# Regrouping the TensorE work of an attention round: both value products together, then every plain float32 matmul, then both fill steps

## Chip, cores and metric

One core of one Trainium2 chip. The metric is the device time of one execution in microseconds (us); of several runs the median is given. A difference is called faster or slower when it is over 0.2% (4.3 us), and no change inside that.

## What is computed

Sink-and-window attention over 4 batches, 8 heads, 768 positions of width 64, then a dense mixture of 8 experts whose gate is normalised over tokens and experts in turn:

```
scores = scale * q @ k.T                      # kept: the first 4 positions, and the last 128
a = softmax(where(keep, scores, -1e9))
x = (a @ v) laid out as 3072 tokens x 512
P = exp(x @ w_gate - max); 8 times: normalise P over experts, then over tokens
out = sum over e of P[:, e] * (relu(x @ w1[e]) @ w2[e])      # F = 1024
```

Everything is float32. Most large products are made as three matmuls in the faster float32r type, from a high part and a low part of each operand; transposes and the gate's products use plain float32.

## The kernel before

The attention is cut into 48 units: 4 batches, 6 blocks of 128 queries, 2 halves of 4 heads. A loop over `n` (L719 on) works on five units at once, each in another state. One turn of that loop is called a round here. TensorE's order in it is the order of the code (`tc.manual_schedule(engines={PE})`); the other engines' orders come from a scheduler, which places their instructions by what TensorE's order makes ready. In a round TensorE does, by line:

- L468, `scores(n + 1)`: 12 float32r matmuls into the PSUM banks `st0` to `st3`, one bank for each head. VectorE adds the mask and takes the maximum (L471), ScalarE takes the exponential (L474), VectorE inverts the sums (L475, L476), GpSimd scales the rows (L478).
- L527, `values(n - 1, 0)` and `values(n - 1, 1)`: 7 float32r matmuls each, into one tile `O` (two PSUM buffers, shared with the gate). `store_x` copies `O` out in two halves, L539, one on ScalarE and one on VectorE, and every second unit stores a block of `x`.
- L433, `transpose_qk(n + 2)`: 4 plain float32 transposes into `st0`. ScalarE copies the high part (L437) and VectorE the low part (L438) into `KQ`, which the next round's scores read.
- L489, `transpose_p(n, 0)` and `(n, 1)`: 8 transposes of the scaled scores into `st1` and `st2`; `split` (L350) copies them out as a high part on ScalarE and a low part on VectorE into `PT`.
- L506, `transpose_sinks(n)`: one transpose into `st3`, copied out by ScalarE (L508).
- `gate_step()`: a quarter of a token tile's gate product, two TensorE passes of 8 columns (L557), with a copy by VectorE (L560) behind the fourth; or, for the first 1024 tokens, a third of a group's product (L568; then a copy `ls`, L573, and eight small passes that read it, L577, and L578).
- `run_fill(1)`: a piece of the mixture's first expert, to fill TensorE's time: either six matmuls of 256 columns (L606), after each second one of which the hidden part is taken by ScalarE (L611) and VectorE (L612), or three of 512 columns (L622). The two kinds take turns.

In a round where the first block of a batch is worked on, there are fewer of L527 and L489, since there is no previous block and no sinks. The fill's weights come by DMA and are split into high and low parts by L350 too (tiles `W1`, `W2f`, `W1f`), in a few rounds. After the attention come the rest of the fill and seven eighths of the mixture, L791, L1035 and L1350, which the change doesn't touch.

The next round's scores need four things: `st0` and `KQ` (L437, L438), `st1` and `st2` (both L350 of each) and `st3` (L508).

Of the kernel before, what the change touches and what calls it, by code (L numbers as in the profile page):

```python
# [229 lines left out]
def tile_sink_attention_moe(ctx: ExitStack, tc: tile.TileContext, q, k, v, wg, w1, w2, out):  # L230
# [4 lines left out]
    E, _, FF = w1.shape  # L235
# [18 lines left out]
    def f32(ap):  # L254
        return ap.bitcast(F32)
# [146 lines left out]
    def load_sinks(b):  # L402
        vs = seq[b] = att.tile([SK, D], F32, name="vs")
        for r0 in range(0, SK, NK):
            (nc.sync if b else nc.scalar).dma_start(vs[r0:r0 + NK, :], v[b, :, 0:SINK, :])

    def split_sinks(b):

        vm = att1.tile([SK, H, D], F32, name="vm")
        nc.gpsimd.tensor_tensor(vm, seq[b].unsqueeze(1).broadcast_to([SK, H, D]), bd.unsqueeze(2).broadcast_to([SK, H, D]), op=ALU.mult)  # L410
        VS = seq[b] = att.tile([SK, H * D], F32R, name="VS")
        vmf = vm.rearrange("p h d -> p (h d)")
        nc.gpsimd.tensor_scalar(VS, vmf, 1.0, 1.0, op0=ALU.mult, op1=ALU.mult)
        nc.gpsimd.tensor_sub(VS[2 * NK:], vmf[2 * NK:], f32(VS[2 * NK:]))

    def load_block(b, i):
        raws[b, i] = r = [att.tile([P, H, D], F32, name=nm) for nm in ("kr", "qr", "vr")]
        cuts = (0, HH, H) if (b, i) == (0, 0) else (0, H)
        for ts in (((r[0], k), (r[1], q)), ((r[2], v),)):
            for h0, h1 in zip(cuts, cuts[1:]):  # L420
                for t, src in ts:
                    nc.sync.dma_start(t[:, h0:h1, :], src[b, h0:h1, i * P:(i + 1) * P, :].rearrange("h p d -> p h d"))
# [88 lines left out]
    def values(n, pr):  # L511

        b, i, hh = units[n]
        u = us[n]
        if pr == 0:
            u["O"] = ps_o.tile([P, NP, 2, P], F32, name="O")
        cs = slice(pr * P, (pr + 1) * P)
        ops = []
        ws = (1,) if i == 0 else (0, 1)
        for j, w in enumerate(ws):  # L520
            V = us[n - 2 + 2 * w]["V"]
            for x_, y_ in ((0, 0), (0, 1), (1, 0)):
                ops.append((V[:, x_, cs], u["PT", pr][:, y_, j]))
        if i:
            ops.append((seq[b][:, hh * HH * D:][:, cs], u["PS"].unsqueeze(1).broadcast_to([SK, 2, P])))
        for j, (x_, y_) in enumerate(ops):
            nc.tensor.matmul(u["O"][:, pr], lhsT=x_, rhs=y_, start=(j == 0), stop=(j == len(ops) - 1))  # L527
        if pr == NP - 1:
            store_x(n)
# [51 lines left out]
    def gate_step():  # L581
        if gates and next(gates[0], 0) == 0:
            gates.pop(0)
            gate_step()
# [76 lines left out]
    def run_fill(k_):  # L661
        for _ in range(k_):
            next(fill, None)
# [53 lines left out]
    START = 5  # L717
    with tc.manual_schedule(engines={PE}):
        for n in range(-2, L + 3):  # L719
            on = lambda j: 0 <= j < L  # L720
            if on(n + 2):
                b, i, hh = units[n + 2]
                if hh == 0:
                    with (tc.high_priority() if n == -2 else nullcontext()):
                        load_block(b, i)
                    if i == 0:
                        load_sinks(b)
            if n == -2:
                nc.sync.dma_start(wg_raw, wg.rearrange("(k p) e -> p k e", p=P))
            if n == 2:  # L730
                with tc.issue_after(us[1]["split"][1]):
                    split_gate()
            gates += later
            later.clear()
            if on(n + 1):
                scores(n + 1, 0)
                scores(n + 1, 1)
            if on(n - 1):
                values(n - 1, 0)
            if n >= START:  # L740
                run_fill(1)
            gate_step()
            for j in (0, 1) if n == -2 else (n + 2,) if n >= 0 else ():
                if on(j):
                    transpose_qk(j)
            if on(n):
                transpose_p(n, 0)
                with (tc.issue_after(us[n - 1]["scaled"]) if n > 1 else nullcontext()):
                    split_v(n)
            gate_step()  # L750
            if on(n):
                transpose_p(n, 1)
            if on(n - 1):
                values(n - 1, 1)
            gate_step()
            if on(n) and units[n][1]:
                transpose_sinks(n)
            if on(n) and units[n][1:] == (0, 1):
                with tc.issue_after(us[n]["scaled"]):
                    split_sinks(units[n][0])  # L760
            if n >= START:
                run_fill(1)
            first_w1(n)
        while gates:
            gate_step()
# [760 lines left out]
```

## Time and profile before

| what | value |
|---|---|
| median of 3 runs | 2140.49 us (2140.0 to 2141.41) |
| profiled execution, its own time | 2140.46 us |
| its span on the core | 2138.7 us |
| TensorE busy, share of the span | 99% |
| VectorE, ScalarE, GpSimd busy | 72%, 41%, 35% |
| mean granted TensorE clock | 0.997 |

Between the span and the execution's own time lie 1.8 us, which no change inside the kernel moves. The rounds of attention fill the stretch from 6.5 to about 298 us. Matmuls are pipelined and their ends are modelled in the profile, so a row's duration holds its neighbour's too: how long something takes on TensorE is read from one start to the next. A wait is listed only where the gap is over 0.15 us.

### The profile page before, as it was taken

To read this page: it belongs to the slowest core of one execution; us is meant where nothing else is said; L and a number is where in the kernel's file an instruction comes from. 1 tells how busy PE (TensorE), PEld (TensorE's weight loads), DVE (VectorE), ACT (ScalarE), POOL (GpSimd) and SP (SyncE) were. 2 spreads that over 40 slices of the span, in tenths; PEclk is the share of its full clock that TensorE was granted. 3 is DMA by queue.
4 is the path that set the end of the run, shared out by engine and by line. 5 is a ranking of instruction groups with operands and counts; after the bars stand their busy time and mean duration, and the time that the engine had idled before them with its cause. 6 is when DMAs were issued, how large, how long until landed. Compare 5 with 4: busy or idle time off the path is not lost.

```text
span 2138.7 us, 31819 instructions
## 1 busy us (share of the span) xinstructions
PE 2120.3 (99%) x10501; PEld 1769.8 (83%) x10501; DVE 1538.8 (72%) x2821; ACT 881.9 (41%) x1867; POOL 750.4 (35%) x950
## 2 busy tenths in 40 slices
PE   8999999999999999999999999999999999999998
PEld 7898897888888888888888888888888888888887
DVE  8878868877777776766666666666657666666666
ACT  7777745444444444442333223332333223332322
POOL 7766643233232331232223222233323232233223
PEclk9999999999999999999999999999999999999999
DMA  7434326999999987686666666667866666666662
GB/s 184 95 84 101 86 80 230 314 307 312 294 309 293 310 290 251 216 282 205 204 192 201 208 192 205 203 200 262 297 204 196 199 207 194 200 207 189 205 197 85
DMA packets 397643, 453.83 MB, mean 212 GB/s; under 512 B 99680, under 2 KB 265760, under 8 KB 396576
## 3 DMA queue, kind: packets, MB, share of 16 engines
q1 hardware_dynamic: 397080, 451.57, 68.0%
q8 instruction: 86, 1.41, 0.3%
q14 instruction: 85, 0.70, 0.1%
q10 hardware_dynamic: 392, 0.16, 0.0%
HBM read 314.17 MB, written 137.46 MB: 211 GB/s over the span
## 4 chain that ended last, share of the span: by engine, by line
PE 94%; DVE 3%; ACT 1%; DMA 1%; issue 0%; POOL 0%; SPq 0%; ACTq 0%; DVEq 0%
PE c L791 40%; PE o L1350 20%; PE held L1350 8%; PE held L1035 7%; PE o L1035 7%; PE O L527 3%; PE st L468 2%; PE st L489 1%; PE o L622 1%; PE g L606 1%; ACT sc L474 1%; PE st L433 1%; DVE sc L471 0%; PE O L557 0%; PE st L606 0%
## 5 line engine op out<-in xcount | busy, mean ns | idle before, releaser
L817 ACT CAST hf<-w 128x512 fp32r<-128x512 f32 x448 | 265.0, 620 | 561.5 <-POOL w L1317 299.2
L1350 PE MATMUL o<-hf,W2q 128*128 128x512 f32 x1920 | 472.0, 389 | 0.0
L1350 PEld LDWEIGHTS o<-hf,W2q 128*128 128x128 f32 x1920 | 360.0, 188 | 75.5 <-DVE acc L1364 0.8
L791 PE MATMUL c<-T,W1q 128*128 128x512 f32 x1530 | 389.0, 389 | 0.2 <-DVE w L1298 0.2
L818 DVE TENSOR_TENSOR hf<-w,hf 128x512 fp32r<-128x512 f32 x448 | 330.4, 766 | 74.3 <-ACT hf L817 66.8
L791 PEld LDWEIGHTS c<-T,W1q 128*128 128x128 f32 x1530 | 286.7, 188 | 60.9 <-DVE w L1298 1.2
L1364 DVE TENSOR_TENSOR acc<-o,acc 128x512 f32<-128x512 f32 x298 | 204.6, 687 | 171.5 <-PE o L1350 171.5
L791 PE MATMUL c<-B,W1q 128*128 128x512 f32 x1134 | 278.3, 389 | 0.0
L1317 POOL TENSOR_TENSOR w<-w 128x512 f32<-128x512 f32 x64 | 82.7, 1292 | 493.2 <-DVE w L1299 486.6
L791 PEld LDWEIGHTS c<-B,W1q 128*128 128x128 f32 x1134 | 212.5, 188 | 44.0
L1298 DVE TENSOR_TENSOR w<-c,M 128x512 f32<-128x512 f32 x192 | 132.3, 689 | 138.8 <-PE c L791 133.1
L1294 ACT COPY M<-c 128x512 f32<-128x512 f32 x192 | 112.7, 587 | 250.4 <-PE c L791 250.3
L1350 PE MATMUL held<-hf,W2q 128*128 128x512 f32 x768 | 194.8, 389 | 0.0
L791 PE MATMUL c<-T,W1f 128*128 128x512 f32 x672 | 171.2, 390 | 0.2
L1035 PE MATMUL held<-W2f,h 128*128 128x512 f32 x672 | 171.1, 390 | 0.0
L1035 PE MATMUL o<-W2f,h 128*128 128x512 f32 x672 | 170.6, 389 | 0.1
L1350 PEld LDWEIGHTS held<-hf,W2q 128*128 128x128 f32 x768 | 144.0, 188 | 29.9
L1332 POOL TENSOR_TENSOR w<-w 128x512 f32<-128x512 f32 x64 | 105.7, 1651 | 176.2 <-DVE hf L818 176.2
L1035 PEld LDWEIGHTS o<-W2f,h 128*128 128x128 f32 x672 | 126.0, 188 | 27.0 <-DVE acc L1042 0.9
L791 PEld LDWEIGHTS c<-T,W1f 128*128 128x128 f32 x672 | 125.7, 188 | 27.1 <-ACT M L998 0.5
L1035 PEld LDWEIGHTS held<-W2f,h 128*128 128x128 f32 x672 | 125.8, 188 | 26.4 <-DVE W2f L818 0.5
L844 POOL TENSOR_TENSOR r<-r 128x256 f32<-128x256 f32 x27 | 20.1, 744 | 359.6 <-ACT M L998 210.0
(216 smaller groups left out, 3100.3 us busy)
## 6 DMA issues: line engine op xcount, KB each, us to landing
W2q<-w2s SPq DMA_DIRECT2D x448, 256.0 KB, 3.2
W1q<-w1s SPq DMA_DIRECT2D x444, 256.0 KB, 2.8
w1s<-W1f SPq DMA_DIRECT2D x56, 896.0 KB, 7.6
w2s<-WT SPq DMA_DIRECT2D x136, 256.0 KB, 3.4
r<-in_moe_w_dram SPq DMA_DIRECT2D x64, 512.0 KB, 4.0
w2s<-W2f SPq DMA_DIRECT2D x56, 256.0 KB, 4.8
PB<-psd SPq DMA_DIRECT2D x16, 512.0 KB, 4.2
w2s<-W2f SPq DMA_DIRECT2D x56, 128.0 KB, 6.5
```

The costliest lines, as they stand in the source:

```text
L468: nc.tensor.matmul(ps[h], lhsT=Q[r0:r0 + D, a, pr, :], rhs=K[r0:r0 + D, c, pr, :], start=(j == 0), stop=(j == 2))
L527: nc.tensor.matmul(u["O"][:, pr], lhsT=x_, rhs=y_, start=(j == 0), stop=(j == len(ops) - 1))
L791: nc.tensor.matmul(ps, lhsT=w1(a, k), rhs=x[:, b, k, :], start=(start and j == 0), stop=(stop and j == len(TERMS) - 1), skip_group_check=n ...
L817: nc.scalar.copy(dst[:, 0], src)
L818: at(1, lambda: nc.vector.tensor_sub(dst[:, 1], src, f32(dst[:, 0])))
L1035: nc.tensor.matmul(o, lhsT=h[c, th][:, a, off:off + P], rhs=W2F[n][:, w, c, :], start=(begin and c == 0 and j == 0), stop=(end and c == 1 ...
L1294: nc.scalar.copy(t, T["c2"])
L1298: nc.vector.tensor_add(w, T["c1"], T[m])
L1317: nc.gpsimd.tensor_sub(S3, T["A11"], T["A21"])
L1332: at(k, lambda: nc.gpsimd.tensor_sub(T["A11"], w, T["A11"]))
L1350: nc.tensor.matmul(o, lhsT=W2Q[part, n, m][:, a, k * P:(k + 1) * P], rhs=F[part, n, H_OF[m]][:, w, :], start=(j == 0 and (begin or not hol ...
L1364: nc.vector.tensor_add(sums[m, k], o, sums[m, k])
```

## The change

In each round `values(n - 1, 1)` moves up behind `values(n - 1, 0)`; the two `transpose_p` follow each other; the three gate steps, which stood at three places of the round, stand in a row behind the transposes; and the two fill steps, of which one stood behind the first values and one at the round's end, both stand at its end. No instruction is added or taken away. The PSUM banks that each use takes are the same.

```diff
             if on(n - 1):
                 values(n - 1, 0)
-            if n >= START:
-                run_fill(1)
-            gate_step()
+                values(n - 1, 1)
             for j in (0, 1) if n == -2 else (n + 2,) if n >= 0 else ():
                 if on(j):
                     transpose_qk(j)
@@
                 transpose_p(n, 0)
                 with (tc.issue_after(us[n - 1]["scaled"]) if n > 1 else nullcontext()):
                     split_v(n)
-            gate_step()
-            if on(n):
                 transpose_p(n, 1)
-            if on(n - 1):
-                values(n - 1, 1)
-            gate_step()
             if on(n) and units[n][1]:
                 transpose_sinks(n)
             if on(n) and units[n][1:] == (0, 1):
                 with tc.issue_after(us[n]["scaled"]):
                     split_sinks(units[n][0])
+            for _ in range(3):
+                gate_step()
             if n >= START:
-                run_fill(1)
+                run_fill(2)
             first_w1(n)
```

TensorE in a round with three gate steps, behind its scores. Before (`st_3397` is the bank for the new K and Q, `st_3404`, `st_3416` and `st_3438` those for the transposed scores and sinks; `g` and `o` are the fill's):

```order
L527 MATMUL O<-PT,V 128x256 x6
L527 MATMUL O<-PS,VS 128x256
L606 MATMUL g_3388<-B_163,W_719 128x256 x2
...
L557 MATMUL O<-wg_raw,xr 128x8
L433 MATMUL st_3397<-ident,kr 128x128
...
L489 MATMUL st_3404<-ident,sc 128x128 x4
L557 MATMUL O<-wg_raw,xr 128x8
L489 MATMUL st_3416<-ident,sc 128x128 x4
L527 MATMUL O<-PT,V 128x256 x6
L557 MATMUL O<-wg_raw,xr 128x8
L506 MATMUL st_3438<-ident,SS_172 96x128
L622 MATMUL o<-W2f,h_2390 128x512 x3
```

And now:

```order
L527 MATMUL O<-PT,V 128x256 x6
L527 MATMUL O<-PS,VS 128x256
L527 MATMUL O<-PT,V 128x256 x6
L527 MATMUL O<-PS,VS 128x256
L433 MATMUL st_3398<-ident,kr 128x128
...
L489 MATMUL st_3405<-ident,sc 128x128 x4
L489 MATMUL st_3416<-ident,sc 128x128 x4
L506 MATMUL st_3427<-ident,SS_172 96x128
L557 MATMUL O<-wg_raw,xr 128x8 x3
L606 MATMUL g_3435<-B_163,W_762 128x256 x2
...
L622 MATMUL o<-W2f,h_2437 128x512 x3
```

The second values moved ahead of all transposes, and the three gate steps (each row of L557 is two passes) became one run between the last transpose and the fill.

VectorE in a round in which a tile's fourth gate step and a split of the fill's weights (`W`) fall, behind the scores' maxima (`st` are the sums of the rows, `h` and `g` the fill's, `KQ`, `PT` and `xr` as above). Before:

```order
L475 TENSOR_SCALAR st<-st 128x2
L476 RECIPROCAL st<-st 128x2
L560 COPY Xt<-O 128x8
L475 TENSOR_SCALAR st<-st 128x2
L476 RECIPROCAL st<-st 128x2
L612 SCALAR_TENSOR_TENSOR h_3183<-g_3388,h_3183 128x256
L350 TENSOR_TENSOR W_3611<-r_3607,W_3611 128x512
L438 TENSOR_TENSOR KQ_174<-st_3503,KQ_174 128x2x2x128
L350 TENSOR_TENSOR PT<-st_3510,PT 128x512
L350 TENSOR_TENSOR PT<-st_3521,PT 128x512
L539 COPY xr<-O 64x256
```

And now:

```order
L475 TENSOR_SCALAR st<-st 128x2
L476 RECIPROCAL st<-st 128x2
L475 TENSOR_SCALAR st<-st 128x2
L476 RECIPROCAL st<-st 128x2
L539 COPY xr<-O 64x256
L438 TENSOR_TENSOR KQ_174<-st_3503,KQ_174 128x2x2x128
L350 TENSOR_TENSOR PT<-st_3510,PT 128x512
L350 TENSOR_TENSOR PT<-st_3521,PT 128x512
L560 COPY Xt<-O 128x8
L612 SCALAR_TENSOR_TENSOR h_3230<-g_3435,h_3230 128x256
L350 TENSOR_TENSOR W_3658<-r_3654,W_3658 128x512
```

VectorE's copy of the values, L539, went from behind the three low parts (L438 and two L350) to a place ahead of them, in all rounds; the gate's copy, the fill's hidden part and the weights' split went the other way. ScalarE's half of L539 also stands ahead of its high parts now.

VectorE in a round in which a group of 512 tokens goes through the gate. Before:

```order
L438 TENSOR_TENSOR KQ_180<-st_1168,KQ_180 128x2x2x128
L350 TENSOR_TENSOR PT<-st_1175,PT 128x512
L573 COPY ls<-O 16x512
L350 TENSOR_TENSOR PT<-st_1196,PT 128x512
L539 COPY xr<-O 64x256
L578 COPY Xt<-O 128x4x8
```

And now:

```order
L539 COPY xr<-O 64x256
L438 TENSOR_TENSOR KQ_180<-st_1161,KQ_180 128x2x2x128
L350 TENSOR_TENSOR PT<-st_1168,PT 128x512
L350 TENSOR_TENSOR PT<-st_1179,PT 128x512
L573 COPY ls<-O 16x512
L578 COPY Xt<-O 128x4x8
```

On TensorE the eight passes that read `ls` (L577) stand right behind the sixteen that make it (L568) now; before, four transposes and seven value matmuls stood between them.

## The prediction

> **What bounds the kernel now.** The page first: busy time by engine, and the chain that ended last.
>
> ```profile
> PE 2120.3 (99%) x10501; PEld 1769.8 (83%) x10501; DVE 1538.8 (72%) x2821; ACT 881.9 (41%) x1867; POOL 750.4 (35%) x950
> PE 94%; DVE 3%; ACT 1%; DMA 1%; issue 0%; POOL 0%; SPq 0%; ACTq 0%; DVEq 0%
> ```
>
> TensorE (PE) is busy for 99% of the span, and 94% of the last chain is its own. Behind the attention its order is unchanged, so what the rounds gain or lose should arrive at the end one for one. The windows of the attention come next (length, then busy us of PE, weight loads, VectorE, ScalarE and GpSimd, granted clock, DMA):
>
> ```profile
> 37.40:122.80 85.40, 84.28 (x706) 76.00 (x706) 69.58 (x250) 65.96 (x209) 62.45 (x143) 1.00 0.42 104
> 122.80:284.10 161.30, 159.74 (x1355) 142.30 (x1354) 134.18 (x476) 121.64 (x378) 103.42 (x242) 1.00 0.36 86
> ```
>
> From 37 us on PE seems always busy, but VectorE is at 82%, so PE's rows may hide short waits. The lengths of rounds tell. Here is PE's timeline (start, length, line); a round is the stretch from one start of L468 to the next.
>
> ```profile
> 70.09 0.98 PE L468 MATMUL st<-KQ 64*128 64x260 f32 x12
> 71.94 0.87 PE L606 MATMUL g<-B,W 128*128 128x256 f32 x6
> 72.64 0.27 PE L433 MATMUL st<-ident,kr 128*128 128x128 f32 x1
> 73.08 1.04 PE L489 MATMUL st<-ident,sc 128*128 128x128 f32 x8
> ...
> 75.69 1.08 PE L468 MATMUL st<-KQ 64*128 64x260 f32 x12
> ...
> 212.06 0.98 PE L468 MATMUL st<-KQ 64*128 64x260 f32 x12
> 213.90 0.87 PE L606 MATMUL g<-B,W 128*128 128x256 f32 x6
> 214.61 0.28 PE L557 MATMUL O<-wg_raw,xr 128*128 128x8 f32 x2
> 215.22 1.04 PE L489 MATMUL st<-ident,sc 128*128 128x128 f32 x8
> 217.84 0.99 PE L468 MATMUL st<-KQ 64*128 64x260 f32 x12
> 223.97 0.99 PE L468 MATMUL st<-KQ 64*128 64x260 f32 x12
> ```
>
> Full rounds that nothing holds up take 5.60 us without a gate step, 5.78 with one and 6.13 with three. Longer ones wait:
>
> ```profile
> 167.84 0.38 PE L468 MATMUL st<-KQ 64*128 64x260 f32 x1
> ...
> 174.80 0.98 PE L468 MATMUL st<-KQ 64*128 64x260 f32 x12
> 180.73 0.39 PE L468 MATMUL st<-KQ 64*128 64x260 f32 x1
> 181.32 1.22 PE L468 MATMUL st<-KQ 64*128 64x260 f32 x11 [0.21 <-DVE PT L350]
> 187.68 0.99 PE L468 MATMUL st<-KQ 64*128 64x260 f32 x12
> ...
> 199.59 0.98 PE L468 MATMUL st<-KQ 64*128 64x260 f32 x12
> ...
> 239.18 0.38 PE L468 MATMUL st<-KQ 64*128 64x260 f32 x1
> 247.20 0.38 PE L468 MATMUL st<-KQ 64*128 64x260 f32 x1 [0.46 <-DVE KQ L438]
> 253.84 0.99 PE L468 MATMUL st<-KQ 64*128 64x260 f32 x12
> ```
>
> Always it is the next scores that wait, for VectorE's low parts. A pair of one round with one step and one with three should take 11.91 (212.06 to 223.97). From 174.80 to 187.68 it took 12.88, from 199.59 to 212.06 12.47, from 239.18 to 253.84 14.66. Together that is 0.97 + 0.56 + 2.75 = 4.3 us over, in rounds in which VectorE splits the fill's weights. The round from 167.84, the first full one of a new batch, has three steps and took 6.96, 0.83 over.
>
> **The change, part by part.** *Moving values, transposes and fill.* A change from float32r to plain float32 or back costs nothing that I can find. L606 to L489 with only L433 between takes 1.14 us (71.94 to 73.08), which is six fill matmuls at 0.118 and four transposes at 0.11. So one change of type fewer in each round is worth 0. Positions hardly matter either: the transposes of the scores start some 2.6 to 3.1 us into a round before and 3.1 us now, as 0.83 us of values replaces 0.7 us of fill.
>
> *Gate steps in a row.* Alone, between L606 and L433, a step adds 0.18 us: 213.90 to 215.22 is 1.32 against 1.14. Two more add 0.35 (6.13 against 5.78). So three cost 0.53 apart. The trace holds one run of three, behind the attention, where no transposes are left:
>
> ```profile
> 298.36 0.73 PE L557 MATMUL O<-wg_raw,xr 128*128 128x8 f32 x6
> 298.94 0.48 PE L606 MATMUL st<-B,W 128*128 128x256 f32 x2
> 299.26 0.86 PE L622 MATMUL o<-W2f,h 128*128 128x512 f32 x3
> ```
>
> From its start to the fill are 0.58 us, and the two fill matmuls behind take 0.32 instead of 0.24: 0.67 in all, 0.14 more than apart. By the same rows a run of one costs 0.14 + 0.08 = 0.22, 0.045 more. A tile has one of each, and there are 16 tiles (128 passes of L557 by eight): 16 x 0.185 = **+2.9 us**. From below it is 0, if a run costs what separate steps do; from above 4, with both differences a third larger.
>
> *The group's gate.* L577 reads `ls`, which VectorE copies from L568's result.
>
> ```profile
> 67.95 0.28 PE L527 MATMUL O<-PS,VS 96*128 96x256 f32 x1
> 68.16 1.05 PE L577 MATMUL O<-sel,ls 16*128 16x8 f32 x8
> ...
> 67.44 0.67 DVE L573 COPY ls<-O 16x512 f32<-16x512 f32 x1
> ```
>
> Before, the copy lay beside 0.5 us of transposes and 0.8 us of values, and PE waited 0.1 us (0.21 between the rows instead of 0.12). Now nothing of PE's stands between: it waits out L568's own end (0.28 from a last start, by the row of L527) and the 0.67 of the copy, with all fill queued behind it: 0.95 instead of 0.2. There are two groups: 2 x 0.75 = **+1.5 us**. From below it is 0.8, if the next rounds win back half; from above 2.5, if VectorE comes to the copy 0.5 late, since it stands behind both L350 now.
>
> *VectorE's order.* Two rounds of its timeline:
>
> ```profile
> 193.73 0.43 DVE L539 COPY xr<-O 64x256 f32<-64x256 f32 x1
> 194.22 0.43 DVE L471 CUSTOM_DVE_ANT_0 sc<-st,mask 128x260 f32<-128x260 f32 x1
> ...
> 197.06 0.17 DVE L476 RECIPROCAL st<-st 128x2 f32<-128x2 f32 x1
> 197.46 0.69 DVE L438 TENSOR_TENSOR KQ<-st,KQ 128x512 fp32r<-128x512 f32 x1 [0.23 <-ACT KQ L437]
> 198.07 1.28 DVE L350 TENSOR_TENSOR PT<-st,PT 128x512 fp32r<-128x512 f32 x2
> ...
> 203.42 0.40 DVE L612 SCALAR_TENSOR_TENSOR h<-g,h 128x256 fp32r<-128x256 f32 x1
> ...
> 204.36 0.68 DVE L438 TENSOR_TENSOR KQ<-st,KQ 128x512 fp32r<-128x512 f32 x1
> ```
>
> The copy L539 takes 0.49 to the next start. In the first of these rounds it now fills VectorE's wait for L437 (0.23 ahead of 197.46), and L438 and both L350 start 0.2 to 0.3 later. They ended at 199.35 (198.07 + 1.28), 0.24 before the next scores (199.59); now they end about when those start. The second L350 empties `st2`, for the second half of the 0.98 that the scores take, so it has nearly 0.5 more; the first, which `st1` needs, ends 0.6 earlier. A round of 5.7 us or more therefore waits for neither. Rounds with a gate step hide it. Those without lose about 0.1, and half of them lost as much before, where L612 stood ahead of L438. It shows where PE has less to do: in the first four rounds, without fill, 0.1 each; and in the three rounds at each new batch, which have half the transposes or half the values, about 0.2 each in nine rounds: together **+2.2 us**. From below it is 0 (L612, 0.32, left the same place in every second round), from above 4, with twice the delay.
>
> ScalarE's cast of `x` for the first 1024 tokens goes the same way, out from behind its high parts; in four full rounds it stands ahead of one L350 now, and it needs VectorE's L539:
>
> ```profile
> 62.25 0.41 ACT L547 CAST B<-xr 128x256 fp32r<-128x256 f32 x1 [0.44 <-DVE xr L539]
> ```
>
> Two of the four are the long group rounds, which hide its 0.41; the others are in the bound of 4. `store_x`'s DMA is issued 2 to 3 us earlier in SP's queue, with the DMA engines at 0.36 to 0.42; GpSimd, 64% busy in the second window, only changes places among the splits of V, the sinks' parts and the scaling, which are needed a round later: 0 for both.
>
> *The weights' splits.* In the round from 199.59 L612 and the split of `W` stand ahead of L438, for 0.94 us (203.42 to 204.36). Both stand behind the low parts now, beside the next scores, and delay the next L471 by about 0.5, which a round of three steps with its 6.3 us takes in. Of the 4.3 us over I take four fifths back: **-3.5 us**. From below (no gain) it is 0, when L471's delay costs as much; the most is -4.3.
>
> The sum: 2.9 + 1.5 + 2.2 - 3.5 = +3.1 us, on the profiled execution's 2140.46 (its span of 2138.7 and 1.8 around it; the median of the runs, 2140.49, is the same). That gives **2143.6 us**, 0.15% longer. A difference under 0.2%, 4.3 us, isn't told from none: from 2136.2 to 2144.8 counts as the same.
>
> [...] In the windows above, the clock was 1.00 in all rounds from 37 us on, which already hold 12 transposes in a row, 1.3 us (four from 72.64, eight from 73.08). In the first rounds plain float32 ran at half the rate:
>
> ```profile
> 16.57 0.42 PE L433 MATMUL st<-ident,qr 128*128 128x128 f32 x1
> 16.78 0.42 PE L433 MATMUL st<-ident,kr 128*128 128x128 f32 x1
> ```
>
> 0.21 from start to start, where it is 0.11 later. [...]
>
> **The rivals.** *A, the low parts become the bound* (slower). With L539 ahead of them and the splits behind, each chain from scores over exponentials, copy and low parts to the next scores takes longer than PE's work in a round. For it speaks that all waits of before end with L438 or L350, and VectorE's 82%. Against it, that a round with gate steps has 5.8 to 6.3 us, and the chain, by the rows of VectorE, 5.7. It decides from where L438 starts more than 0.4 us later than before. Then nothing of the 4.3 comes back, the rounds without gate steps lose 0.25 each (8 of them, 2 us), and the new batches cost 4: 2.9 + 1.5 + 4 + 2 = +10.4, **2150.9 us**; half of it gives 2147. *B, waits vanish and runs are free* (faster). If a run of gate steps costs what steps cost apart, the groups cost their least (0.8), and all waits go, at weights (4.3) and at the first two new batches (0.83 as at 167.84, and the same for the one before it), it is 0.8 - 4.3 - 1.7 = -5.2, **2135.3 us**. For it speaks that VectorE's heavy rows leave the place ahead of L438; against it the measured run at 298.36. *C, the clock*: if the run of plain float32 halved the clock for its own time, 12 transposes would take 0.11 more each, 1.3 us a round, over 46 rounds +60, **2204 us**. Against it stands the granted 1.00.
>
> **How the numbers follow.** The sum has 0.62, and its own range is 2140 to 2146.5; over 2144.8 lies 0.09 of that. A has 0.25, nearly all of it over 2144.8. B has 0.11, 0.06 of it under 2136.2. C has 0.02. So faster 0.06, same 0.60, slower 0.34. The range that leaves out 2 in 10 goes from 2138.5, into B, to 2150, into A.
>
> **What would show it.** Right would be: runs of L557 x6 with 0.67 us to the fill's second matmul; rounds of 5.82 and 6.27 us; a gap of nearly 1 us on PE ahead of L577, released by L573; no wait at the rounds with `W`; L539 on VectorE right behind the second L476, and L438 0.2 to 0.3 us later in the round. Wrong would be: waits of L468 for L350 in most rounds (A), an unchanged 5.78 and 6.13 (B), a granted clock under 1.00 after 40 us (C), or a difference that lies behind 300 us.

## The result, and the profile after

The changed kernel takes **2154.22 us** (median of 6 runs, 2152.44 to 2155.42) against 2140.26 before: a ratio of 1.0064, with a 95% interval of 1.0053 to 1.0075. It is slower by 14 us, where 3 were forecast, and lies above the range.

The page of the profile after, busy time by engine and the chain that ended last:

```profile
PE 2128.3 (99%) x10501; PEld 1776.7 (83%) x10501; DVE 1539.3 (72%) x2821; ACT 878.2 (41%) x1867; POOL 749.1 (35%) x950
PE 94%; DVE 3%; ACT 2%; issue 1%; POOL 0%; DMA 0%; POOLq 0%; DVEq 0%; ACTq 0%
```

It reads as it did before: 99% and 94%. Where the 14 us are can't be seen there. The lengths of the rounds show it (called by the loop's `n`; round 6 begins at 43.91 us before and at 48.73 after). Summed by stage, from one start of L468 to another:

| rounds | before, us | after, us | more | forecast |
|---|---|---|---|---|
| up to round 6 (from 6.5) | 37.4 | 42.2 | 4.8 | 0.4 |
| two with a group's gate, and the one behind the second | 23.1 | 27.1 | 4.0 | 1.5 |
| new batches (from 81.4, 152.8 and 224.0) | 58.7 | 61.7 | 3.0 | 2.4 |
| splits of weights (from 174.8 and 239.2) | 58.1 | 59.3 | 1.2 | -2.7 |
| the others | 100.4 | 102.5 | 2.1 | 1.0 |

(The forecast's column spreads its terms over the stages, the runs of gate steps with 0.185 for each pair of rounds; 0.4 of them lie behind the attention.) The sum is 15.2; 14.5 of it still stand at the last matmul and 13.9 at the end of the span. Nothing of the loss comes from behind the attention.

TensorE's timeline after, in rounds that nothing holds up (start, length, line):

```profile
225.19 0.98 PE L468 MATMUL st<-KQ 64*128 64x260 f32 x12
229.30 0.29 PE L557 MATMUL O<-wg_raw,xr 128*128 128x8 f32 x2
229.44 0.96 PE L606 MATMUL g<-B,W 128*128 128x256 f32 x6
231.03 0.99 PE L468 MATMUL st<-KQ 64*128 64x260 f32 x12
235.13 0.73 PE L557 MATMUL O<-wg_raw,xr 128*128 128x8 f32 x6
235.72 0.96 PE L606 MATMUL g<-B,W 128*128 128x256 f32 x6
237.31 0.86 PE L468 MATMUL st<-KQ 64*128 64x260 f32 x10
```

5.84 and 6.28 us for 5.78 and 6.13: the runs of gate steps cost 0.21 for a pair, near the 0.185 of the forecast. Now the first rounds, on the same timeline:

```profile
27.19 0.38 PE L468 MATMUL st<-KQ 64*128 64x260 f32 x1 [2.31 <-DVE KQ L438]
...
36.83 0.88 PE L527 MATMUL O<-PT,V 128*128 128x256 f32 x6
...
38.98 0.27 PE L506 MATMUL st<-ident,SS 128*96 128x128 f32 x1
40.69 0.39 PE L468 MATMUL st<-KQ 64*128 64x260 f32 x1 [1.44 <-DVE KQ L438]
...
43.57 1.48 PE L527 MATMUL O<-PT,V 128*128 128x256 f32 x6
```

Behind the last transpose of a round (38.98) TensorE has nothing until the next scores, which wait 1.44 us, and 2.31 two rounds before. And the same six matmuls take 0.88 in one round and 1.48 in the next. The windows of the profile say why (length, busy time of PE, weight loads, VectorE, ScalarE, GpSimd, granted clock, DMA):

```profile
26.06:29.47 3.41, 2.06 (x16) 1.54 (x17) 3.35 (x9) 2.46 (x7) 3.32 (x8) 1.00 0.38 101
29.47:32.88 3.41, 3.41 (x18) 3.41 (x18) 2.48 (x12) 2.41 (x10) 2.24 (x6) 0.50 0.67 152
32.88:43.12 10.24, 8.09 (x65) 6.53 (x64) 9.45 (x30) 8.55 (x24) 7.16 (x17) 1.00 0.76 200
43.12:46.53 3.41, 3.41 (x18) 3.41 (x17) 2.64 (x15) 2.62 (x10) 1.74 (x5) 0.50 0.25 54
46.53:125.04 78.51, 74.96 (x620) 67.13 (x619) 60.40 (x209) 55.81 (x180) 54.03 (x123) 1.00 0.41 96
125.04:128.45 3.41, 3.41 (x19) 2.66 (x19) 0.00 (x0) 0.00 (x0) 0.00 (x0) 0.50 0.04 9
```

Behind 26 us three stretches of 3.41 us in the attention ran at half the clock, 0.50, where TensorE is busy all the time and does the work of 1.7 us. Two follow the long waits of the first rounds, 2.31 and 1.44 us. The kernel before has half clock in its first rounds too, for 6.8 us, and none in the rest of the attention:

```profile
20.99:27.81 6.82, 5.78 (x27) 4.98 (x29) 6.76 (x25) 5.14 (x16) 4.57 (x12) 0.50 0.35 75
```

The third stretch after the change follows the wait of the second group:

```profile
120.76 2.14 PE L568 MATMUL O<-B,wgr 128*128 128x256 f32 x16
123.76 1.02 PE L577 MATMUL O<-sel,ls 16*128 16x8 f32 x8 [0.86 <-DVE ls L573]
```

At a new batch one more thing appears. TensorE's wait, then VectorE's and GpSimd's timelines ahead of it:

```profile
98.90 0.84 PE L468 MATMUL st<-KQ 64*128 64x260 f32 x5 [1.45 <-DVE KQ L438]
```

```profile
95.54 0.56 DVE L475 TENSOR_SCALAR st<-st 128x2 f32<-128x2 f32 x1
96.14 0.17 DVE L476 RECIPROCAL st<-st 128x2 f32<-128x2 f32 x1
96.53 0.93 DVE L475 TENSOR_SCALAR st<-st 128x2 f32<-128x2 f32 x1 [0.23 <-ACT sc L474]
97.69 0.43 DVE L539 COPY xr<-O 64x256 f32<-64x256 f32 x1
98.15 0.69 DVE L438 TENSOR_TENSOR KQ<-st,KQ 128x512 fp32r<-128x512 f32 x1
```

```profile
95.34 0.73 POOL L448 TENSOR_TENSOR V<-vr,V 128x256 fp32r<-128x256 f32 x1
96.15 1.28 POOL L414 TENSOR_TENSOR VS<-vm,VS 32x512 fp32r<-32x512 f32 x1
```

L475 adds a constant to 128x2 numbers, usually in 0.17 us. Here it takes 0.56 and 0.93, and ends at 96.10 and 97.46, 0.03 behind L448 (96.07) and L414 (97.43) of GpSimd. The copy L539 then stands ahead of L438 with its 0.46. The three delays, 0.39, 0.76 and 0.46, come to 1.6 us, a little more than the wait.

In a round with splits, ScalarE's and VectorE's timelines:

```profile
206.17 0.62 ACT L350 CAST W1f<-r 128x512 fp32r<-128x512 f32 x1 [1.28 <-DMA r<-in_moe_w_dram]
206.69 0.38 ACT L611 ACTIVATE h<-g 128x256 fp32r<-128x256 f32 x1
```

```profile
207.10 0.42 DVE L612 SCALAR_TENSOR_TENSOR h<-g,h 128x256 fp32r<-128x256 f32 x1 [1.18 <-ACT h L611]
207.45 0.68 DVE L350 TENSOR_TENSOR W1f<-r,W1f 128x512 fp32r<-128x512 f32 x1
208.04 0.42 DVE L471 CUSTOM_DVE_ANT_0 sc<-st,mask 128x260 f32<-128x260 f32 x1
211.05 0.43 DVE L539 COPY xr<-O 64x256 f32<-64x256 f32 x1
211.51 0.69 DVE L438 TENSOR_TENSOR KQ<-st,KQ 128x512 fp32r<-128x512 f32 x1
```

ScalarE's cast of new weights waits for their DMA; L611 stands behind it, L612 waits for L611, and L471 stands behind L612. From L471 to the end of L438 are 4.16 us, and the next scores, which could start at 212.17, start at 212.25 and then wait for L350.

### The profile page after: what moved, and what is told of

It reads as the page before. It is cut to its first block, busy times and chain, and to the rows that moved or that the text cites. A ratio compares the mean times of both kernels' runs of the same rounds, so it can differ in the third digit from the quotient of the medians.

```text
span 2152.6 us, 31806 instructions
## 1 busy us (share of the span) xinstructions
PE 2128.3 (99%) x10501; PEld 1776.7 (83%) x10501; DVE 1539.3 (72%) x2821; ACT 878.2 (41%) x1867; POOL 749.1 (35%) x950
## 4 chain that ended last, share of the span: by engine, by line
PE 94%; DVE 3%; ACT 2%; issue 1%; POOL 0%; DMA 0%; POOLq 0%; DVEq 0%; ACTq 0%
PE c L786 40%; PE o L1345 20%; PE held L1345 8%; PE held L1030 7%; PE o L1030 7%; PE O L527 3%; PE st L468 2%; PE g L606 1%; PE o L622 1%; PE st L489 1%; ACT sc L474 1%; PE st L433 1%; PE st L606 0%; PE O L622 0%; DVE KQ L438 0%
## 5 line engine op out<-in xcount | busy, mean ns | idle before, releaser
L1312 POOL TENSOR_TENSOR w<-w 128x512 f32<-128x512 f32 x64 | 82.7, 1293 | 492.4 <-DVE w L1294 492.4
L1327 POOL TENSOR_TENSOR w<-w 128x512 f32<-128x512 f32 x64 | 105.7, 1652 | 176.0 <-DVE hf L813 176.0
L1316 POOL TENSOR_TENSOR w<-w 128x512 f32<-128x512 f32 x64 | 83.9, 1311 | 176.2 <-DVE w L1294 174.8
```

Of the source, the lines that this page charges most:

```text
L1312: nc.gpsimd.tensor_sub(S3, T["A11"], T["A21"])
L1316: nc.gpsimd.tensor_add(T["A21"], T["A21"], T["A22"])
L1327: at(k, lambda: nc.gpsimd.tensor_sub(T["A11"], w, T["A11"]))
```

## The experiments

Sixteen kernels, in the order in which they ran. A difference is that of medians, to the kernel before beside which they ran (2140.3 to 2140.6); the changed kernel's is +14.0. What an edit takes off the changed kernel is the difference of the two kernels' own medians, from 2154.22. Rows, round lengths and the clock come from one profiled execution of each kernel.

### The parts alone

The first kernel puts all the values ahead in the kernel before:

```diff
                 values(n - 1, 0)
+                values(n - 1, 1)
...
-            if on(n - 1):
-                values(n - 1, 1)
             gate_step()
```

> The kernel before, with one part of the change: the second half of the values stands right behind the first; fill and gate steps stay where they were before. VectorE's copy L539 so stands ahead of L438 and both L350 in every round. Theory 1 (this copy lengthens the chain from scores over exponentials, copy and low parts to the next scores, and the waits that it opens in the first rounds and at the new batches also bring back stretches of half clock): +6 to +9 us on before, about 2148, most of it before 50 us and in the rounds behind each new batch, with a second stretch of half clock after 28 us. Theory 2 (the loss comes from the splits of weights and L612, now behind the low parts): at most +2, since they stand ahead here. Theory 3 (from the gate steps in a row): at most +2.

2164.72 us: **+24.4**, a ratio of 1.0112 (1.0096 to 1.0127). This is almost three times the most that any theory had. Nearly every full round is longer by 0.3 to 0.9 us, not only those of the first theory.

The second puts the gate steps in a row, in the kernel before:

```diff
-            gate_step()
...
+            for _ in range(3):
+                gate_step()
             if n >= START:
                 run_fill(1)
```

> The kernel before, with one part of the change: the three gate steps in a row behind the transposes of the sinks, ahead of the second fill step; values and fill stay where they were. Theory 3 (runs of L557 cost 0.22 us for each of 16 tiles, 3.5 us, and PE waits 0.9 us more in each of two groups, with one stretch of half clock worth 1.7 us where the wait falls badly): +5 to +7 us, about 2146. Theory 1 and 2: at most +3, as the copy L539 and the splits stay where they were.

2146.05: **+5.8**, ratio 1.0027 (1.0017 to 1.0038), as the theory of the gate steps had it. The group rounds are 1.06 and 0.96 longer, each pair of rounds 0.2, and one stretch of half clock (70.7 to 74.2 us, granted 0.51) costs 1.4.

The third puts the fill at the end, in the kernel before:

```diff
-            if n >= START:
-                run_fill(1)
             gate_step()
...
             if n >= START:
-                run_fill(1)
+                run_fill(2)
```

> The kernel before, with one part of the change: both fill steps at the end of a round. L612 and the splits of weights go behind the low parts; the copy L539 stays behind them too. Forecast's step (the waits of 4.3 us in the rounds with splits go): -3.5, about 2137. Theory 2 (splits and L612 behind the low parts push the next L471 back and cost as much as they free): 0 to +2. Theory 1 and 3: no loss, so 0 or less.

2139.81: **-0.5**, ratio 0.9997 (0.9988 to 1.0006), no difference that can be told. The rounds from 180.7 and 205.4 fall from 6.95 and 6.70 to 6.35 and 6.12, and another rises from 6.13 to 7.76. Its rows, on TensorE's timeline and then on VectorE's:

```profile
195.99 0.33 PE L433 MATMUL st<-ident,kr 128*128 128x128 f32 x1 [1.47 <-DVE st L471]
```

```profile
194.56 0.42 DVE L612 SCALAR_TENSOR_TENSOR h<-g,h 128x256 fp32r<-128x256 f32 x1 [1.76 <-ACT h L611]
195.51 0.42 DVE L471 CUSTOM_DVE_ANT_0 sc<-st,mask 128x260 f32<-128x260 f32 x1
```

It is what the changed kernel shows at 207.10: L612 waits for ScalarE, and the next scores' L471 stands behind it.

The parts alone add up to +29.7, the whole change to +14: they are not independent. In the first run one piece of fill was left ahead of the transposes; in the changed kernel both stand behind them.

The fourth kernel is the changed one with VectorE's copy held back:

```diff
-        if pr == NP - 1:
-            store_x(n)
...
                 transpose_p(n, 1)
+            if on(n - 1):
+                with (tc.issue_after(us[n]["split"][1]) if on(n) else nullcontext()):
+                    store_x(n - 1)
```

> The changed kernel, with TensorE's order left as it is, but the copies of the values written behind the transposes and VectorE's held behind the second low part (L350): VectorE does L438, both L350, then the copy, as before; splits and L612 stay behind. Theory 1: the 7 to 8 us of the first rounds, the new batches and the rounds with splits come back, leaving runs of gate steps and the group's wait: 2146 to 2148, no half clock between 28 and 100 us. Theory 2 or 3: 2152 or more.

2149.35: **+9.1**, so 4.9 of the 14 go, less than the first theory wanted. Half clock came nevertheless, from 27.6 and from 123.2 us. Round 6 starts at 45.86. The six rounds from 183.9 take 36.5 us, for 37.9 in the changed kernel and 37.3 before: here the splits behind the low parts do pay. But the group's copy `ls` now waits behind the held copy: the gap ahead of L577 is 1.49 instead of 0.86. Of the 2.9 us that are won by round 6, 1.6 are round 5, which has no half clock here (6.47 for 8.04).

### What the waits cost

A fill step between the second and the third gate step, in group rounds of the changed kernel:

```diff
+            group = bool(gates) and gates[0].gi_code.co_name == "gate_group"
-            for _ in range(3):
-                gate_step()
+            gate_step()
+            gate_step()
+            if group:
+                run_fill(1)
+            gate_step()
             if n >= START:
-                run_fill(2)
+                run_fill(1 if group else 2)
```

> The changed kernel; in the two rounds of a group's gate one fill step stands between the second and the third gate step, so that TensorE has 0.8 us to do while VectorE copies ls. If the wait of 0.86 us ahead of L577 and the stretch of half clock behind the second group are the group's cost: -0.8 for each wait and -1.7 for the stretch, 3 us less than the changed kernel, 2150.8 to 2151.5. If the rounds behind (low parts late) set the time anyway: within 1 us of the changed kernel's 2154.2.

2152.82: **+12.2**. The group rounds fall from 9.85 and 11.16 to 9.22 and 9.23 and the one behind from 6.12 to 5.59, 3.1 us in all, as expected, and the first rounds, which the edit doesn't touch, are 1.1 shorter, with a stretch of half clock fewer. Only 1.4 arrive: two new stretches, from 98.9 and from 259.4 us, lengthen a round by 1.4 and 1.5 each. These rounds have the same waits in the changed kernel (1.45 us ahead of 98.90, 0.96 ahead of 261.45) and ran there at the full clock, 1.00.

The gate steps back among the transposes, the rest as changed:

```diff
                 values(n - 1, 1)
+            gate_step()
...
+            gate_step()
+            if on(n):
                 transpose_p(n, 1)
+            gate_step()
...
-            for _ in range(3):
-                gate_step()
```

> The changed kernel with the three gate steps put back between the transposes; values stay in a row and fill at the end. If the gate steps in a row cost here what they cost when put into the kernel before (+5.8): 2148 to 2149. If the wait and the run of gate steps give VectorE time that the copy L539 then uses, so that the parts hide one another: 2151 or more.

2150.53: **+10.0**, so 3.7 of the 14 are the gate steps', between the two expectations. The group rounds stay at 9.89: with the values in a row the last gate step has nothing ahead of it even so.

The changed kernel without L475:

```diff
-        nc.vector.tensor_scalar(rs[:, p2], sm[:, p2], 1e-9, None, op0=ALU.add)
-        nc.vector.reciprocal(rs[:, p2], rs[:, p2])
+        nc.vector.reciprocal(rs[:, p2], sm[:, p2])
```

> The changed kernel without L475, which adds 1e-9 to sums of exponentials of at least 1 (a sum that float32 rounds back to the same number); L476 reads the sums directly. In the changed kernel L475 took 0.56, 0.93, 1.17 and 1.17 us instead of 0.17 at 95.5, 96.5, 171.9 and 245.1 us, ending with an instruction of GpSimd each time. If these delays make the waits of 1.45, 0.31 and 0.3 us ahead of L468 there, they go, and each round's chain is 0.34 shorter besides: -2 to -5 us, 2149 to 2152. If GpSimd only happens to end then, or L476 is held instead: within 1 us of 2154.2.

2148.95: **+8.4**, so 5.3 go, a little more than expected. VectorE's rows where L475 took 0.56 and 0.93 (the reciprocal has its line number here), and GpSimd's:

```profile
93.63 0.17 DVE L475 RECIPROCAL st<-st 128x2 f32<-128x2 f32 x1
94.62 0.17 DVE L475 RECIPROCAL st<-st 128x2 f32<-128x2 f32 x1 [0.83 <-ACT sc L474]
```

```profile
93.42 1.28 POOL L414 TENSOR_TENSOR VS<-vm,VS 32x512 fp32r<-32x512 f32 x1
```

The reciprocal takes its 0.17 in the middle of L414. The round of the wait of 1.45 falls from 5.96 to 4.89, and the rounds with splits from 6.61, 6.72 and 6.65 to 6.28, 6.28 and 6.09. The six rounds of the changed kernel in which an L475 took over 0.25 us lose 3.3 us in all. The three rounds with splits hold no such L475 and still lose 1.3: there the ordinary time of the two additions counts.

The changed kernel with work for TensorE in the waits of the first rounds (L759, read by nothing):

```diff
+            if n in (1, 2, 4):
+                spare = bank1([P, GH])
+                for _ in range({1: 6, 2: 10, 4: 6}[n]):
+                    nc.tensor.matmul(spare[:, 0:P], lhsT=ident, rhs=ident, start=True, stop=True)
```

> The changed kernel with 6, 10 and 6 plain float32 matmuls of 128x128 into a spare bank, read by nobody, at the end of the rounds that begin at 13.8, 20.4 and 34.1 us, where TensorE waits 1.3, 2.3 and 1.4 us. If these waits bring the stretches of half clock from 29.5 and 43.1 us: the stretches go, and 2 to 3.4 us with them, 2151 to 2152, though TensorE does more. If the clock costs nothing there (VectorE's low parts set those rounds anyway): 2154 or more.

2152.52: **+11.9**. Its window over the first rounds, in which the changed kernel had two stretches at 0.50:

```profile
27.00:49.00 22.00, 20.45 (x170) 18.08 (x170) 20.73 (x75) 18.15 (x57) 16.45 (x38) 1.00 0.80 189
```

The clock stays at 1.00, round 6 starts at 45.68, 3.05 earlier, though TensorE did more. Round 3 takes 5.86 us for 6.95, round 5 6.48 for 8.04. Round 4 stays at 6.61. Then a stretch at 259 us takes 1.5 back, so 1.7 arrive.

### Copy or cover

The kernel before without L475, as a control:

> The kernel before without L475, the addition of 1e-9 to the sums; L476 reads the sums. In before L475 is stretched at 93.9 (0.58), 94.9 (0.42) and 231.6 us (1.28), ahead of the waits of L468 at 96.5 (0.31) and 234.0 us (0.10). If the stretched L475 makes those waits and those of the rounds with splits nearly as long: -1 to -3 us, 2137.5 to 2139.5. If the 5.3 us that the same edit took off the changed kernel come only with the copy L539 in the chain: within 0.7 us of before.

2139.57: **-1.0**, ratio 0.9997 (0.9988 to 1.0006), not told from none, between the expectations. L475 takes as long there (21.8 us in the attention; 22.8 after the change). The same addition costs some 1 us in one order and 5 in the other.

The run of +24.4 again, with VectorE's copy held behind the low parts (the edit of the fourth kernel):

> The kernel before with all values ahead of the transposes (as in the run that was 24.4 us slower), and the copies of the values written behind the transposes, VectorE's held behind the second low part. TensorE's order is that of the slower run; VectorE's is that of before. Theory 1 (the place of the copy L539 on VectorE makes the loss): 2140 to 2144. If the loss comes of TensorE's own order (transposes later in the round, nothing of PE's left behind them): 2155 or more.

2162.28: **+21.7**. The theory of the copy falls for that run: only 2.4 come back. Rows of one of its rounds, from TensorE, ScalarE and VectorE:

```profile
61.00 0.90 PE L604 MATMUL g<-B,W 128*128 128x256 f32 x6
61.73 0.27 PE L433 MATMUL st<-ident,kr 128*128 128x128 f32 x1
63.07 0.95 PE L604 MATMUL g<-B,W 128*128 128x256 f32 x6
63.95 1.61 PE L468 MATMUL st<-KQ 64*128 64x260 f32 x12
```

```profile
62.37 0.59 ACT L437 CAST KQ<-st 128x512 fp32r<-128x512 f32 x1
```

```profile
62.98 0.69 DVE L438 TENSOR_TENSOR KQ<-st,KQ 128x512 fp32r<-128x512 f32 x1 [0.58 <-ACT KQ L437]
63.59 1.28 DVE L350 TENSOR_TENSOR PT<-st,PT 128x512 fp32r<-128x512 f32 x2
```

VectorE waits for L437, and L437 starts (62.37) when the transposes L433 end (the last from 62.06 to 62.33). Both halves of the values and one fill step stand ahead of them. Behind all the transposes (63.07) TensorE has 0.88 us of fill. The way from the transposes over L437, L438 and both L350 ends at 64.87 (63.59 + 1.28), while TensorE comes to the next scores at 63.95 and waits in them (1.61 for twelve that take 0.98 where nothing holds them up). In this order the transposes come late, and the work left behind them doesn't cover that way.

Fill at the end and no L475, both in the kernel before:

> The kernel before with both fill steps at the end of a round, and without L475. Fill at the end alone gave -0.5; the rounds with splits gained, and one round behind a late W1f lost 1.6. If the two edits add up: 2137 to 2138.5, faster than both kernels. If the stalls of VectorE behind GpSimd are hidden in this order anyway: 2139 to 2140.

2137.68: **-2.9**, ratio 0.9991 (0.9982 to 1.0000). The two edits add up. The rounds with splits from 174.5 take 35.7 us for 37.3, with no wait left.

The changed kernel with copy, gate steps and L475 all undone:

> The changed kernel with values in a row and fill at the end, but with gate steps apart, the copy held behind the second low part, and without L475. If copy, gate steps and the stretched L475 are all of the changed kernel's loss: 2138 to 2141, no more than before. If something else of TensorE's order costs (the group's wait, clock in the first rounds): 2142 to 2145.

2144.70: **+4.2**. Something else costs, as its second expectation said: round 6 starts 2.6 us late, 1.5 of it from a stretch of half clock in round 5 (7.99 for 6.54), and the group rounds are 1.1 and 0.9 longer. Behind the second of them it is 1.0 faster than before.

The changed kernel with the values of the first rounds back behind the transposes:

```diff
                 values(n - 1, 0)
-                values(n - 1, 1)
+                if n >= START:
+                    values(n - 1, 1)
...
                 transpose_p(n, 1)
+            if on(n - 1) and n < START:
+                values(n - 1, 1)
```

> The changed kernel, but in the rounds without fill (the first ones, to 40 us) the second half of the values stands behind the transposes, as before the change; all later rounds as changed. Theory 4 (what TensorE has behind the transposes covers the way transposes, high copies, low parts, next scores; the first rounds have nothing there once the values go ahead, wait, and lose the clock as well): the 4.8 us that the changed kernel is behind by 48.7 us go, 3.5 to 5 in all, 2149 to 2151. Theory 1 alone (the copy L539 in front of L438, wherever the values stand): no more than 1.5 us come back.

2150.25: **+9.9**, so 4.0 go, and round 6 starts at 44.30. It doesn't part cover from copy cleanly: with the values later, the scheduler puts VectorE's copy back behind the low parts too in these rounds. Nor does it part them from the clock: its half clock, 6.8 us from 21.4, lies where that of the kernel before lies. In the fourth kernel, with the copy alone held back, rounds 1 and 4 are back to 6.02 and 5.81 (5.98 and 5.64 before), and 1.6 of the 1.9 us that stay by round 6 are round 3, at half clock there (6.93 for 5.30).

Values of the first rounds back, gate steps apart, and no L475, together:

> The changed kernel with three things undone or taken out together: values of the first rounds back behind the transposes, gate steps apart, no L475 (the addition of 1e-9). The copy L539 stays ahead of L438 in all later rounds, values stay in a row and fill at the end. If cover in the first rounds (4 us), gate steps (3.7) and the stretched L475 with its share of the chain (5.3) are separate causes of the 14: 2140 to 2142. If they overlap (the same waits counted twice): 2143 to 2146.

2142.21: **+1.9**, ratio 1.0009 (1.0000 to 1.0018). One by one these took off 4.0, 3.7 and 5.3, 13.0 in all; together they take off 12.0. The causes overlap little, as far as stretches of half clock, which come and go with each edit, let one tell. The 1.9 left are a sum: the two group rounds take 9.76 and 9.91 for 8.77 and 8.70, with a wait of 0.85 ahead of L577, a stretch of half clock from 250.7 us costs 1.6, and the first rounds are 1.1 shorter than before, as they are (1.0) in the control without L475.

### The waits that the forecast counted twice

The two longest rounds with splits (8.02 and 6.64 from 239.2 us before) were as long in nearly every run, wherever VectorE's splits stood. On ScalarE's and GpSimd's timelines of before:

```profile
243.34 0.62 ACT L350 CAST W1f<-r 128x512 fp32r<-128x512 f32 x1 [2.51 <-POOL r L691]
243.87 0.51 ACT L474 ACTIVATE sc<-sc,st 128x260 f32<-128x260 f32 x1
```

```profile
244.07 1.20 POOL L692 TENSOR_TENSOR r<-r,r 128x256 f32<-128x256 f32 x1
```

ScalarE's cast of the first streamed weights waits 2.5 us for GpSimd's sums, and the round's exponentials stand behind it. Two kernels hold these splits behind the low parts of the last four rounds, the first of them on top of the fastest kernel so far:

```diff
-            split(*first_pieces.pop(0))
+            with ExitStack() as held_back:
+                for ins in us[min(n, L - 1)]["split"]:
+                    held_back.enter_context(tc.issue_after(ins))
+                split(*first_pieces.pop(0))
```

> The kernel before with fill at the end of a round, without L475 (the addition of 1e-9), and with the four splits of the first streamed weights (W1f) held behind the low parts of the last four rounds, so that ScalarE's cast does not stand, waiting for GpSimd's sums, ahead of a round's exponentials. Should the loss of the rounds from 237 to 259 us (8.07, 6.61 and 6.64 for 6.12, 5.79 and 6.12) come of that wait: 2135 to 2136.5, some 4 us less than before. If these rounds wait for something else: 2137 to 2138.5, like the run without the hold.

2136.90: **-3.6**, ratio 0.9983 (0.9974 to 0.9992). It is the only one whose interval lies below that of no change, though by less than the 0.2% set at the start, and 0.8 better than without the hold, between the two expectations.

> The kernel before with that hold alone (splits of W1f behind the low parts of the last four rounds; fill, values, gate steps and L475 as before). The forecast put 2.75 us of the rounds from 239.2 to 253.8 us down to where VectorE's splits of the fill's weights stand. If it is ScalarE's and VectorE's wait for the sums instead, these rounds lose 1.5 to 2.5 us although the fill's splits stay: 2138 to 2139. If the forecast's reading was right: 2140 or more.

2141.28: **+0.8**, ratio 1.0003 (0.9994 to 1.0012). By its time this is the second expectation. By its rows the two rounds lose 1.1 us (7.46 and 6.07), less than the first expectation had, with the fill's splits where they were: a part of those 2.75 us was this wait. A later round pays 0.7 of it, 6.83 for 6.13, and 0.9 is lost behind the attention's last scores. What holds the first of the two at 7.46 was not settled.

## Why the prediction was wrong

**The first rounds** are where the forecast failed first. Its term was "the first four rounds, without fill, 0.1 each", with the clock at nothing. They became 4.8 us by round 6, and two things are in it.

The order on VectorE and ScalarE makes 2.1: rounds 1, 3 and 4 are longer by 0.64, 0.56 (5.86 for 5.30, with the clock at 1.00) and 0.91. In round 4 L438 starts 5.81 us behind the start of the scores (34.14 to 39.95) where it started 4.91 behind (31.73 to 36.64). The copy L539 now stands ahead of it, and a split of the fill's weights ahead of L471 (35.43). The transposes are not late there: TensorE's last L433 starts at 38.00 and ScalarE's L437 at 38.88, behind the exponentials and ScalarE's half of the copy. So TensorE's wait shows where it has nothing to do, but VectorE sets the length of the round.

Half clock makes the other 2.6: round 3 takes 6.95 us where it takes 5.86 at 1.00, and round 5 8.04 where it takes 6.48. The kernel before loses nothing by its own half clock, which lies in round 2 (6.81 us; 6.83 in the kernel of -3.6, at 1.00 from 20.1 us on). In round 3 a stretch costs the kernel of -2.9 1.1 us too (6.59 for 5.45 in the kernel of -3.6), with the values where they stood before. So some of the 4.8 is luck, since it depends on which round a stretch meets.

**Positions hardly matter** holds for rounds at the full clock in the changed kernel, where both fill steps went behind the transposes. It doesn't hold in general: with one fill step left ahead of them the same move of the values cost 24.4 us. Nor does it hold at half clock. Rows of round 3 after the change, from TensorE, ScalarE and VectorE:

```profile
32.32 0.42 PE L433 MATMUL st<-ident,qr 128*128 128x128 f32 x1
32.78 0.59 ACT L437 CAST KQ<-st 128x512 fp32r<-128x512 f32 x1 [0.49 <-PE st L433]
33.40 0.69 DVE L438 TENSOR_TENSOR KQ<-st,KQ 128x512 fp32r<-128x512 f32 x1 [0.65 <-ACT KQ L437]
```

L438 waits for L437, and L437 for the transposes, which stand behind both value products. In the rounds behind this stretch and the next one no L437 waits for them (38.88 and 52.31).

**VectorE's order** was right in kind: L539 stands ahead of L438 in every round, and rounds of full length hide it. Its size was not: holding it back gave 4.9 us, with one stretch of half clock fewer, against a term of 2.2. The forecast added its 0.2 to 0.3 to a chain with room. It missed that the copy takes the room that other delays need: L475 costs 1.0 us before, which is not told from none, and 5.3 with the copy in the chain.

**The weights' splits** gave -3.5 on paper, and +0.3 when the 0.9 us of gate steps in those rounds is taken from the 1.2 measured. Two errors are in it. Of the 4.3 us, 2.75 were read from the lengths of two rounds, and at least 1.1 of that is ScalarE's wait for GpSimd's sums, which the order of the fill's splits doesn't touch. And "a round of three steps with its 6.3 us takes in" the later L471 fails twice: L612 stands ahead of L471 as well and can wait for ScalarE, and the chain from L471 has no 0.5 to spare once the copy is in it. With the copy behind, the six rounds from 174.8 do win: 1.5 us of the 1.53 that were counted there, in the kernel with fill at the end and no L475.

**Gate steps in a row**: 0.21 a pair for 0.185, so 3.4 us for 2.9. Right.

**The group's gate**: the wait of 0.86 (forecast 0.95) stands in both groups, released by L573. Right for the wait; the second group also lost its clock for 3.41 us, which makes 1.8 of the 2.5 that are over (11.16 for the 9.85 of the first group, and 6.12 for 5.63 in the round behind).

**The rivals.** A came nearest with 2150.9, though not by its own sign: most scores wait for L438, at new batches and first rounds, not for L350 in most rounds. C was dismissed because the clock was 1.00 from 37 us on, with 12 transposes in a row. Its sign came true, a clock of 0.50 after 40 us (from 43.12 and 125.04), but not its mechanism. The run of plain float32, now with gate steps, brings no half clock by itself: it stands in all the rounds of the 78.51 us at 1.00. Waits come before each stretch: with work in those of the first rounds both stretches are gone (3.05 us by round 6), and with a fill step in the group's wait the third is. The second recurs in three other kernels with these waits open (from 40.9, 41.1 and 41.2 us), the first in only one of them. So a forecast that opens waits here has to price them twice, with a range for where the stretch falls. Each of the three stretches lasts 3.41 us. No wait was longer than 2.31 us, and in the 3.41 us ahead of the first stretch TensorE was busy for 2.06. Which waits bring a stretch was not shown.

## What to carry to other kernels

When an engine's work is regrouped, look at the queues of the other engines too. A product that moves ahead takes its copy with it, ahead of the work for which the next round waits, and rounds without filler show it first (2.1 us in rounds 1, 3 and 4). The producer of the next round's input has to come early, with enough work behind it to cover the way back (where it came late, +24.4 us, and +21.7 with the copy held back). Read a wait by the row that is late, on every engine back to the first one, before a change is credited with removing it. A chain with a few tenths of slack hides stalls of the same size, until something else takes that slack (L475: 1.0 us before, 5.3 with the copy in the chain).

## What had not been expected of the hardware

An addition on VectorE over 128x2 float32 numbers, from SBUF to SBUF, took up to 1.28 us (before, at 231.6 us) where its usual time is 0.17. Before and after the change 20 of them in all took over 0.25 us; 18 of these end 0.02 to 0.03 us after an instruction of GpSimd has ended, the other two 0.05 and 0.09 us after one. Not every addition beside GpSimd is held: some beside L478 took 0.17 (after, at 38.75, with an L478 from 38.70 to 39.19). The reciprocal over the same numbers never took more than 0.17. VectorE's groups of the attention after the change (count, busy us, mean ns):

```profile
L475 DVE TENSOR_SCALAR st<-st 128x2 f32<-128x2 f32 x96 | 22.8, 238 | 27.7 <-ACT sc L474 23.5
L476 DVE RECIPROCAL st<-st 128x2 f32<-128x2 f32 x96 | 15.8, 165 | 3.1
```

Why the addition is held and the reciprocal isn't was not shown.

Half clock followed some waits and not others. After the change the three stretches stand behind waits of 2.31, 1.44 and 0.86 us (ahead of 27.19, 40.69 and 123.76). Waits of 1.35 us ahead of 20.38, 0.86 ahead of 73.51, 1.45 ahead of 98.90 and 0.96 ahead of 261.45 brought none there, with the clock at 1.00 behind them; at the last of them, near 259 us there, a stretch cost 1.5 us in two other kernels. What decides was not shown.
